# A Strassen scheme for the down projection of a TensorE-bound attention and MLP-Mixer kernel

## The chip, the cores and the metric

The kernel runs on one core of one Trainium2 chip. The metric is the device time of that core in microseconds. Spans and waits come from a profiled execution, which is some 2 us shorter than the timed figure (304.3 us of span beside 306.4 us of time). Runs are compared when their granted TensorE clock says that they are in the same state.

## The reference

Eight batches go through block-causal attention (8 heads, 576 positions, head width 64) and then through one MLP-Mixer layer: a token mix across positions and a channel mix with an inner width of 1536.

```python
x  = attention(q, k, v)                       # [8, 576, 512]
h  = relu(x.T @ w_tok1) @ w_tok2              # token mix, per batch
u  = x + h.T
h2 = relu(u @ w_ch1) @ w_ch2                  # channel mix: 512 -> 1536 -> 512
out = u + h2                                  # float32
```

The last product, `relu(...) @ w_ch2`, is the **down projection**. Per batch it is [512 rows x 1536] @ [1536 x 512]; the last 64 rows of two neighbouring batches are handled together as a "pair" of 128 rows ("mixed" in the code).

## The kernel before: what the change touches

The kernel first makes a list of operations, each with its engines, an assumed cost, its dependencies and the buffers it takes. A planner replays this list on a small model of the engines, moves priorities at random 1000 times from a fixed seed, keeps what ends earliest, and then emits every engine's instructions in the order found, with semaphore waits where one needs another engine's result. So an edit to the list of operations also starts the search anew.

```python
def search(self, tries):
    rnd = random.Random(0)
    ...
    for _ in range(tries):
        moved = list(prios)
        ...
        end = run(moved)[0]
        if end <= best:
            best, prios = end, moved
    return run(prios)[1]
```

The channel mix keeps the hidden activations transposed, `gT` = [128 partitions, 12 channel chunks, 512 rows], which makes them the stationary operand of the down projection. Each chunk of 128 rows is 12 matmuls of 512 columns, accumulated in one PSUM bank, and one eviction by VectorE that adds the residual:

```python
for n, si in enumerate(chunks):               # 4 chunks of 128 rows
    ...
    for cols in (slice(0, 256), slice(256, 512)) if last else (slice(0, 512),):
        ...
        for part in range(3):
            ...
            for cc in range(4 * part, 4 * part + 4):
                nc.tensor.matmul(
                    out=ps, lhsT=gt[:, cc, c0 : c0 + 128], rhs=wc2_sb[:, cc, cols],
                    start=(cc == 0 and not turned), stop=(cc == NDC - 1),
                )
        ...
        nc.vector.tensor_tensor(
            out=dst, in0=ps, in1=(ut if mixed else ut[:, si, :])[:, cols], op=ADD
        )
```

Batch 0 differs ("turned"): its residual is added on TensorE by identity matmuls in the same bank. The program sets up four "mm" banks of PSUM for all of this and two double banks for attention's scores.

The softmax here doesn't subtract the row's maximum and nothing guards it: scores larger than these inputs give would overflow.

## Time and profile before

| | before |
|---|---|
| time, median of runs | 306.38 us (306.02 to 306.77) |
| span of the profiled run | 304.3 us |
| TensorE busy | 296.9 us, 98% |
| VectorE busy | 155.5 us, 51% |
| ScalarE busy | 164.6 us, 54% |
| granted TensorE clock | 1.000 |

The page's other lines are in the prediction. How they are read: a digit of the slices is the busy share of a fortieth of the span in tenths; a group has line, engine, operation, tiles and shapes, then the count, busy time and mean ns of one, then the engine's idle time before it and what ended that.

### The profile page before, as it was taken

The numbers are of one execution on the slowest core, as the hardware profiler recorded it, in microseconds if no ns is written. First come the engines' busy times: TensorE is split into PE (matmuls) and PEld (weight loads), VectorE is DVE, ScalarE is ACT, GpSimd is POOL, SyncE is SP. The second block draws the span as 40 slices with busy tenths as digits, with TensorE's granted clock in tenths as the row PEclk, the third lists the DMA queues.
The fourth block names the chain that finished last, engine by engine and source line by source line (L and its number), as shares of the span: only waits on it lengthen the run. The fifth ranks groups of instructions, "written<-read, shape, count | busy, mean of one in ns | idle before, by whom it ended". The sixth has DMA issues, their size and how long they took to land.

```text
span 304.3 us, 7056 instructions
## 1 busy us (share of the span) xinstructions
PE 296.9 (98%) x2999; PEld 160.7 (53%) x3034; DVE 155.5 (51%) x380; ACT 164.6 (54%) x233; POOL 62.1 (20%) x96
## 2 busy tenths in 40 slices
PE   8999999999999999999999999999999999999995
PEld 4575456465454564555554564645446545555443
DVE  5566539989595599584987253615023021010112
ACT  5887855677855756875557856324413503615300
POOL 9766454702610602600140000000000000000000
PEclk9999999999999999999999999999999999999999
DMA  8999999995982998975193002033113222100133
GB/s 202 179 196 209 200 191 187 220 216 91 142 121 44 161 119 139 189 46 60 54 107 88 2 2 53 18 95 97 36 32 140 46 80 49 43 26 2 69 138 106
DMA packets 64383, 31.94 MB, mean 105 GB/s; under 512 B 53088, under 2 KB 55008, under 8 KB 64352
## 3 DMA queue, kind: packets, MB, share of 16 engines
q0 software_dynamic: 44320, 17.34, 48.9%
q1 hardware_dynamic: 19744, 13.57, 17.1%
q10 hardware_dynamic: 288, 0.59, 0.5%
q8 instruction: 23, 0.38, 0.5%
q14 instruction: 8, 0.07, 0.1%
HBM read 35.85 MB, written 9.44 MB: 149 GB/s over the span
## 4 chain that ended last, share of the span: by engine, by line
PE 95%; DMA 2%; issue 1%; DVE 1%; ACT 0%; ACTq 0%
PE mm L1031 31%; PE mm L947 28%; PE mm L555 10%; PE sc L508 10%; PE mm L736 6%; PE mm L829 4%; PE mm L974 4%; DMA gT<-in_q_dram 2%; PE mm L860 1%; PE mm L332 1%; PE mm L780 0%; PE mm L910 0%; DVE qT L393 0%; PE mm L1023 0%; PE mm L765 0%
## 5 line engine op out<-in xcount | busy, mean ns | idle before, releaser
L527 ACT ACTIVATE e_sb<-sc 128x1024 bf16<-128x1024 f32 x95 | 92.5, 1028 | 26.3 <-PE sc L508 24.5
L947 PE MATMUL mm<-uT,wc_sb 128*128 128x512 bf16 x384 | 91.2, 380 | 0.1
L1031 PE MATMUL mm<-wc_sb,gT 128*128 128x512 bf16 (+1 forms) x372 | 89.4, 372 | 1.5 <-issue 0.5
L722 ACT ACTIVATE gT<-mm 128x512 bf16<-128x512 f32 x74 | 44.2, 597 | 63.1 <-PE mm L947 62.8
L947 PEld LDWEIGHTS <-wc_sb 128*128 128x128 bf16 x384 | 41.9, 114 | 39.3 <-issue 3.9
L1031 PEld LDWEIGHTS <-gT 128*128 128x128 bf16 x396 | 36.9, 98 | 40.8 <-issue 3.3
L1056 DVE TENSOR_TENSOR o_sb<-mm,u_sb 128x512 f32<-128x512 f32 (+1 forms) x29 | 19.5, 672 | 74.5 <-PE mm L1031 74.3
L422 POOL DMA_DIRECT2D v<-in_v_dram x45 | 37.2, 839 | 35.3 <-PE sc L508 23.6
L508 PE MATMUL sc<-qT,kT 32*128 32x64 bf16 (+4 forms) x744 | 35.4, 281 | 0.5 <-DVE qT L393 0.5
L555 PEld LDWEIGHTS <-e_sb 128*128 128x128 bf16 x896 | 31.1, 97 | 8.0 <-issue 3.6
L555 PE MATMUL mm<-v,e_sb 128*128 128x65 bf16 x896 | 33.9, 193 | 0.1
L583 DVE TENSOR_TENSOR x_sb<-mm,rinv 128x320 bf16<-128x320 f32 x64 | 31.0, 491 | 2.0
L724 DVE TENSOR_SCALAR gT<-mm 128x512 bf16<-128x512 f32 x22 | 15.2, 689 | 15.9 <-PE mm L947 15.7
L844 DVE TENSOR_TENSOR u_sb<-mm,x_sb 128x512 bf16<-128x512 f32 x28 | 18.0, 686 | 10.2 <-PE mm L829 9.0
L393 DVE STREAM_TRANSPOSE qT<-qraw 128x288 int32<-128x288 int32 x32 | 21.6, 706 | 3.0 <-PE sc L508 2.1
L393 DVE STREAM_TRANSPOSE kT<-kraw 128x288 int32<-128x288 int32 x32 | 20.9, 703 | 4.3 <-DMA kraw<-in_k_dram 1.7
L508 PEld LDWEIGHTS <-kT 32*128 32x128 bf16 x752 | 12.3, 93 | 19.8 <-issue 16.7
L736 PE MATMUL mm<-x_sb,w_sb 128*128 128x512 bf16 (+1 forms) x98 | 18.0, 314 | 0.3
L533 DVE MEMSET e_sb<- 64x128 uint32 (+1 forms) x72 | 10.5, 153 | 14.7 <-ACT e_sb L527 11.4
L373 POOL DMA_DIRECT2D qraw<-in_q_dram x15 | 8.3, 552 | 42.2 <-DVE qT L393 28.5
L577 DVE RECIPROCAL rinv<-mm 128x5 f32<-128x5 f32 x64 | 11.4, 185 | 7.4 <-PE mm L555 6.7
L722 ACT ACTIVATE aT<-mm 128x512 bf16<-128x512 f32 (+1 forms) x15 | 8.1, 543 | 12.3 <-PE mm L736 12.3
(66 smaller groups left out, 175.6 us busy)
## 6 DMA issues: line engine op xcount, KB each, us to landing
out_dram<-o_sb SPq DMA_DIRECT2D x15, 512.0 KB, 2.9
kraw<-in_k_dram POOLq DMA_DIRECT2D x15, 288.0 KB, 7.7
qraw<-in_q_dram POOLq DMA_DIRECT2D x15, 288.0 KB, 7.2
v<-in_v_dram POOLq DMA_DIRECT2D x28, 128.0 KB, 6.9
wc_sb<-in_moe_w_ch_dram POOLq DMA_DIRECT2D x8, 192.0 KB, 7.1
wc_sb<-in_moe_w_ch_dram POOLq DMA_DIRECT2D x3, 512.0 KB, 10.4
out_dram<-o_sb SPq DMA_DIRECT2D x10, 128.0 KB, 2.3
v<-in_v_dram POOLq DMA_DIRECT2D x15, 64.0 KB, 6.1
```

Source lines behind the costliest of these rows:

```text
L393: nc.vector.transpose(dst[:, 0:S, :] .rearrange("p s e -> p (s e)") .bitcast(I32) .rearrange("p (a k) -> p k a", k=NB)[:, k0:k1], raw2.bit ...
L422: nc.gpsimd.dma_start(out=dst, in_=src)
L508: nc.tensor.matmul(out=home(n)[:, c0 : c0 + w], lhsT=kT[i][r, j0 : j0 + 128, par], rhs=qT[i][r, i0 : i0 + w, par], start=(par == 0), stop= ...
L527: nc.scalar.activation(dst, sc[SC.index(note["pool"])][:, :, 0:n], EXP, scale=scale)
L555: nc.tensor.matmul(out=u[:, I, 0:65], lhsT=w, rhs=vt[:, J, head, 0:65], start=(J == 0), stop=(J == I),)
L583: nc.vector.tensor_tensor(out=xt[:, :, 64 * head : 64 * head + 64], in0=u[:, :, 0:64], in1=ri.to_broadcast([128, 5, 64]), op=MULT,)
L722: nc.scalar.activation(dst, src, RELU)
L736: nc.tensor.matmul(out=bank_of(bank)[:, w * n : w * n + w], lhsT=wt[:, tt : tt + 255 : 2], rhs=xt[:, c, cols], start=(c == 0), stop=(c == 4),)
L844: nc.vector.tensor_tensor(out=ut[:, si, :], in0=bank_of(bank), in1=xt[:, si, :], op=ADD)
L947: nc.tensor.matmul(out=bank_of(bank), lhsT=wc1_sb[:, m, channels(cc)], rhs=uT[b % 2][:, :, m, :], start=(m == 0), stop=(m == NDM - 1),)
L1031: nc.tensor.matmul(out=ps, lhsT=gt[:, cc, c0 : c0 + 128], rhs=wc2_sb[:, cc, cols], start=(cc == 0 and not turned), stop=(cc == NDC - 1),)
L1056: nc.vector.tensor_tensor(out=dst, in0=ps, in1=(ut if mixed else ut[:, si, :])[:, cols], op=ADD)
```

## The change

The intent is to give TensorE less to do. Chunks t and t+2 of a batch (rows 128t and 128t+256) are taken as two row blocks, the channels as two halves of 768, the output columns as two halves of 256. That is a 2 x 2 by 2 x 2 block product, which Strassen's scheme (in Winograd's form) does in 7 block products, not 8:

- sums of activations, on VectorE, per chunk pair: s1 = a21 + a22, s2 = s1 - a11, s4 = a12 - s2, s3 = a11 - a21 (s3 in place of a21);
- differences of weights, on VectorE, once: w1 to w4;
- seven products of 6 matmuls with 256 columns each;
- three PSUM banks: in bank "a" four products pile up one after the other, and after each of them VectorE folds the bank's present content into one quarter of the output tile; bank "e" holds two products, bank "c" one.

The residual is added in the first fold of each quarter, from the chunk pair's own rows. Batches 1 to 7 are changed; batch 0 and the pairs are not. With the new tiles, two rings of the pairs (`umT`, `gmT`) shrank from two buffers to one each, and the zeros for the filler matmuls in the first 16 us moved into the new weights' tile.

The diff, cut to its core (the rest changes buffer indices):

```diff
-    umT = ring(2, [128, NDM, 128], BF16, "umT")
+    umT = ring(1, [128, NDM, 128], BF16, "umT")
-    gmT = ring(2, [128, NDC, 128], BF16, "gmT")
+    gmT = ring(1, [128, NDC, 128], BF16, "gmT")
+    sums = ring(3, [128, 3, NDC // 2, 128], BF16, "sums")
-    zeros = sb.tile([128, 512], BF16, name="zeros")
+    wd_sb = sb.tile([128, 4, NDC // 2, 256], BF16, name="wd_sb")
+    zeros = wd_sb[:, 0, 0:2, :].rearrange("p c s -> p (c s)")
+    def weight_sums(wc2_ready):
+        ...                                    # 4 differences of [128, 6, 256]
+    def channel_down_fast(b, g_done, wc2_ready, u_done, prio):
+        for t in range(2):
+            ...
+            for key, dst, x, y, op in (
+                ("s1", s1, a21, a22, ADD), ("s2", s2, s1, a11, SUB),
+                ("s4", s4, a12, s2, SUB), ("s3", a21, a11, a21, SUB),
+            ):
+                def emit(o, dst=dst, x=x, y=y, op=op):
+                    nc.vector.tensor_tensor(out=dst, in0=x, in1=y, op=op)
+            ...
+            def product(n, to, x, y, deps):
+                bank, first = banks[to], to not in last
+                def emit(o):
+                    for kk in range(H6):
+                        nc.tensor.matmul(
+                            out=bank_of(bank)[:, 0:256], lhsT=x[:, kk], rhs=y[:, kk],
+                            start=first and kk == 0, stop=kk == H6 - 1, ...
+                        )
+                # waits for the fold before it in the same bank: deps + [last.get(to)]
+            def fold(to, row, col, op, residual, final):
+                other = ut[:, t + 2 * row, cols] if residual else dst
+                nc.vector.tensor_tensor(out=dst, in0=bank_of(bank)[:, 0:256], in1=other, op=ADD)
+            fold("a", 0, 0, product(0, "a", a11, b11, []), True, False)
+            fold("e", 1, 1, product(1, "e", s1, w1_, [made["s1"]]), True, False)
+            fold("a", 0, 1, product(2, "a", s2, w2_, [made["s2"]]), True, False)
+            fold("e", 0, 1, product(3, "e", s4, b22, [made["s4"]]), False, True)
+            fold("a", 1, 1, product(4, "a", a21, w3_, [made["s3"]]), False, False)
+            fold("c", 0, 0, product(5, "c", a12, b21, []), False, True)
+            fold("a", 1, 0, product(6, "a", a22, w4_, []), True, True)
-            if p < B - 1:
+            if p == 0:
                 channel_down(p, ...)
+            elif p < B - 1:
+                channel_down_fast(p, ...)
```

More of the change, by code (lines that the diff above doesn't have):

```diff
@@ L19 @@
 MULT = mybir.AluOpType.mult
+SUB = mybir.AluOpType.subtract
 class Op:
@@ L897, in emit @@
             def emit(o):
-                nc.sync.dma_start_transpose(out=umT[pair % 2], in_=umt)
-            op = P.add("SP", 1.0, emit, um_rows + reuse(("umT", pair % 2)), prio, xfer=1.0)
+                nc.sync.dma_start_transpose(out=umT[0], in_=umt)
+            op = P.add("SP", 1.0, emit, um_rows + reuse(("umT", 0)), prio, xfer=1.0)
             reads(("um", pair % 2), op)
@@ L914, in token_mix @@
             deps = ([u_done[si]] if si < 4 else um_rows) + pads["ident"]
-            deps += uT_war if si < 4 else reuse(("umT", pair % 2))
+            deps += uT_war if si < 4 else reuse(("umT", 0))
             op = P.add(
@@ L922, in emit @@
                 ps = bank_of(bank).bitcast(BF16)[:, 0:512].rearrange("p (m s) -> p m s", m=NDM)
-                dst = uT[b % 2][:, si] if si < 4 else umT[pair % 2]
+                dst = uT[b % 2][:, si] if si < 4 else umT[0]
                 if o.engine == "ACT":
@@ L964, in channel_up_mixed @@
     def channel_up_mixed(pair, umT_done, wc1_ready, prio):
-        g_war = reuse(("gm", pair % 2))
+        g_war = reuse(("gm", 0))
         done = []
@@ L976, in emit @@
                             lhsT=wc1_sb[:, m, channels(cc)],
-                            rhs=umT[pair % 2][:, m, :],
+                            rhs=umT[0][:, m, :],
                             start=(m == 0),
@@ L982, in channel_up_mixed @@
             op = P.add("PE", mm_cost(128, 16), emit, umT_done + wc1_ready[4 * f] + g_war, prio + 0.1 * f, take=[(BANK, bank)])
-            reads(("umT", pair % 2), op)
+            reads(("umT", 0), op)
             def emit(o, f=f, bank=bank):
@@ L987, in emit @@
                     o,
-                    gmT[pair % 2][:, 4 * f : 4 * f + 4, :],
+                    gmT[0][:, 4 * f : 4 * f + 4, :],
                     bank_of(bank).rearrange("p (c s) -> p c s", c=4),
@@ L993, in channel_up_mixed, with emit @@
         return done
+    H6 = NDC // 2
+    wd_ready = []
+    def weight_sums(wc2_ready):
+        b11, b12 = wc2_sb[:, 0:H6, 0:256], wc2_sb[:, 0:H6, 256:512]
+        b21, b22 = wc2_sb[:, H6:NDC, 0:256], wc2_sb[:, H6:NDC, 256:512]
+        t = [wd_sb[:, n] for n in range(4)]
+        for dst, x, y, deps in (
+            (t[0], b12, b11, wc2_ready), (t[2], b22, b12, wc2_ready), (t[1], b22, t[0], []), (t[3], b21, t[1], [])
+        ):
+            def emit(o, dst=dst, x=x, y=y):
+                nc.vector.tensor_tensor(out=dst, in0=x, in1=y, op=SUB)
+            wd_ready.append(P.add("DVE", 0.9, emit, deps + wd_ready[-1:], 14.0))
@@ new lines, in channel_down_fast, with emit @@
+    def channel_down_fast(b, g_done, wc2_ready, u_done, prio):
+        gt, ut = gT[b % 2], u_sb[b % 3]
+        for t in range(2):
+            oi = out_n[0] % 3
+            out_n[0] += 1
+            o_war = reuse(("o", oi))
+            si = sum_n[0] % 3
+            sum_n[0] += 1
+            s_war = reuse(("s", si))
+            r1, r2 = slice(128 * t, 128 * t + 128), slice(128 * t + 256, 128 * t + 384)
+            a11, a12 = gt[:, 0:H6, r1], gt[:, H6:NDC, r1]
+            a21, a22 = gt[:, 0:H6, r2], gt[:, H6:NDC, r2]
+            s1, s2, s4 = (sums[si][:, n] for n in range(3))
+            made = {}
+            prev = None
+            for key, dst, x, y, op in (
+                ("s1", s1, a21, a22, ADD), ("s2", s2, s1, a11, SUB), ("s4", s4, a12, s2, SUB), ("s3", a21, a11, a21, SUB),
+            ):
+                def emit(o, dst=dst, x=x, y=y, op=op):
+                    nc.vector.tensor_tensor(out=dst, in0=x, in1=y, op=op)
+                prev = made[key] = P.add(
+                    "DVE", dve_cost(768, 2), emit, (g_done + s_war if prev is None else [prev]), prio - 2 + 0.1 * t
+                )
+                reads(("g", b % 2), prev)
+            b11, b21, b22 = wc2_sb[:, 0:H6, 0:256], wc2_sb[:, H6:NDC, 0:256], wc2_sb[:, H6:NDC, 256:512]
+            w1_, w2_, w3_, w4_ = (wd_sb[:, n] for n in range(4))
+            banks = {"a": {}, "c": {}, "e": {}}
+            last = {}
+            stored = []
+            def product(n, to, x, y, deps):
[4 more added lines that the diff above has]
+                            out=bank_of(bank)[:, 0:256], lhsT=x[:, kk], rhs=y[:, kk],
+                            start=first and kk == 0, stop=kk == H6 - 1,
+                            skip_group_check=not first,
+                        )
+                op = P.add(
+                    "PE", mm_cost(256, H6), emit, deps + g_done + wc2_ready + wd_ready + [last.get(to)],
+                    prio + 0.2 * t + 0.02 * n, take=[(BANK, bank)] if first else (),
+                )
+                reads(("g", b % 2), op)
+                reads(("s", si), op)
+                last[to] = op
+                return op
+            def fold(to, row, col, op, residual, final):
+                dst = o_sb[oi][:, row, 256 * col : 256 * col + 256]
+                bank = banks[to]
+                other = ut[:, t + 2 * row, 256 * col : 256 * col + 256] if residual else dst
+                def emit(o):
+                    nc.vector.tensor_tensor(out=dst, in0=bank_of(bank)[:, 0:256], in1=other, op=ADD)
+                done = P.add(
+                    "DVE", dve_cost(256), emit, [op, folded.get((row, col))] + u_done + o_war, prio - 1,
+                    give=[bank] if final else (),
+                )
+                reads(("u", b % 3), done)
+                folded[row, col] = last[to] = done
+                return done
+            folded = {}
+            fold("a", 0, 0, product(0, "a", a11, b11, []), True, False)
[5 more added lines that the diff above has]
+            fold("a", 1, 0, product(6, "a", a22, w4_, []), True, True)
+            rows = out[b, 0:512, :].rearrange("(c t p) d -> t p c d", c=2, t=2)[t]
+            if b == B - 1 and t == 1:
+                pieces = [(0, 0, 2), (1, 1, 2), (1, 0, 1)]
+            else:
+                pieces = [(None, 0, 2)]
+            for row, c0, c1 in pieces:
+                def emit(o, row=row, c0=c0, c1=c1, oi=oi, rows=rows):
+                    cols = slice(256 * c0, 256 * c1)
+                    if row is None:
+                        nc.sync.dma_start(out=rows, in_=o_sb[oi])
+                    else:
+                        nc.sync.dma_start(out=rows[:, row, cols], in_=o_sb[oi][:, row, cols])
+                deps = [folded[r, c] for r in ((0, 1) if row is None else (row,)) for c in range(c0, c1)]
+                size = (2 if row is None else 1) * (c1 - c0) / 2
+                reads(("o", oi), P.add("SP", 0.5, emit, deps, prio, xfer=8 * 0.086 * size))
@@ L995 @@
     out_n = [0]
+    sum_n = [0]
     def channel_down(b, g_done, wc2_ready, u_done, prio, mixed=False):
         chunks = [None] if mixed else list(range(4))
-        gt = gmT[b // 2 % 2] if mixed else gT[b % 2]
+        gt = gmT[0] if mixed else gT[b % 2]
         ut = um_sb[b // 2 % 2] if mixed else u_sb[b % 3]
@@ L1046, in channel_down @@
                     )
-                reads(("gm", b // 2 % 2) if mixed else ("g", b % 2), prev)
+                reads(("gm", 0) if mixed else ("g", b % 2), prev)
                 if turned:
@@ L1098 @@
     wc1_ready, wc2_ready = load_channel_weights()
+    weight_sums(wc2_ready)
     x_done = {}
@@ L1112 @@
             g_done = channel_up(p, uT_done, wc1_ready, 10 * p + 2)
-            if p < B - 1:
+            if p == 0:
                 channel_down(p, g_done, wc2_ready, u_done, 10 * p + 4)
+            elif p < B - 1:
+                channel_down_fast(p, g_done, wc2_ready, u_done, 10 * p + 4)
             if p % 2 == 1:
@@ L1119 @@
             if p == B - 1:
-                channel_down(p, g_done, wc2_ready, u_done, 10 * p + 4)
+                channel_down_fast(p, g_done, wc2_ready, u_done, 10 * p + 4)
     with tc.manual_schedule():
```

## The prediction

No row of the kernel before shows the new sums, so their times in the prediction are estimates. The same figures can be worked out from rows of that kernel, the 690 and 424 ns of 512 and 256 f32 columns in the prediction and these two:

```profile
L355 DVE COPY o_sb<-mm 128x512 f32<-128x512 f32 x2 | 1.4, 691 | 0.1
L927 DVE COPY uT<-mm 128x512 bf16<-128x512 bf16 x3 | 1.2, 422 | 1.1 <-PE mm L910 1.1
```

From 690 and 424 ns an f32 column takes (690 - 424)/256 = 1.039 ns, and 158 ns come on top. The bf16 copy of 512 columns takes 422 ns, as long as 256 f32 columns: double rate. If the bf16 sums show it too, 768 columns take an estimated 158 + 384 x 1.039 = 557 ns and 1536 take 956; at single rate 768 take 956.

> **What bounds the kernel now.** I read first the busy shares and the 40 slices of the page, then the chain that ended last, then the groups with shapes kept apart, then the waits of TensorE alone and the timeline of the end.
>
> Busy shares, slices, chain and the waits of TensorE alone, from the kernel before:
>
> ```profile
> PE 296.9 (98%) x2999; PEld 160.7 (53%) x3034; DVE 155.5 (51%) x380; ACT 164.6 (54%) x233; POOL 62.1 (20%) x96
> ...
> PE   8999999999999999999999999999999999999995
> ...
> DVE  5566539989595599584987253615023021010112
> ...
> PEclk9999999999999999999999999999999999999999
> ...
> PE 95%; DMA 2%; issue 1%; DVE 1%; ACT 0%; ACTq 0%
> ...
> PE mm L1031 <- issue: 0.5, 3, 0.2
> PE sc L508 <- DVE qT L393: 0.5, 1, 0.5
> ```
>
> TensorE (PE) is busy 98% of the 304.3 us span in every slice but the first and last, makes up 95% of the chain, and, after its start, waited for another engine under 1 us in all. Its clock was 1.000. So the kernel takes as long as TensorE's instruction stream: a microsecond out of that stream is a microsecond off the time, as long as no new wait appears. VectorE (DVE) is half busy on the average, but the slices show two different halves: mostly 5 to 9 tenths up to slice 25 (attention still running), 0 to 3 after. That matters below.
>
> The groups that the change touches (line, engine, operation, tiles, shapes, count | busy us, mean ns), and rows of the timeline (start, us):
>
> ```profile
> L1031 PE MATMUL mm<-wc_sb,gT 128*128 128x512 bf16 x348 | 86.6, 379 | 1.5 <-issue 0.5
> L1031 PE MATMUL mm<-wc_sb,gT 128*128 128x256 bf16 x24 | 2.8, 272 | 0.0
> L1056 DVE TENSOR_TENSOR o_sb<-mm,u_sb 128x512 f32<-128x512 f32 x27 | 18.6, 690 | 73.0 <-PE mm L1031 72.8
> L1056 DVE TENSOR_TENSOR o_sb<-mm,u_sb 128x256 f32<-128x256 f32 x2 | 0.8, 424 | 1.5 <-PE mm L1031 1.5
> ```
>
> ```profile
> 209.08 5.34 PE L947 MATMUL mm<-uT,wc_sb 128*128 128x512 bf16 x24
> ...
> 298.18 2.78 PE L1031 MATMUL mm<-wc_sb,gT 128*128 128x256 bf16 x24
> ...
> 301.00 0.42 DVE L1056 TENSOR_TENSOR o_sb<-mm,u_sb 128x256 f32<-128x256 f32 x1 [0.89 <-PE mm L1031]
> ```
>
> A matmul's mean of 379 or 272 ns is its latency, not its cost: they are pipelined. The pace comes from runs. 24 matmuls of 512 columns took 5.34 us: (5.34 - 0.379)/23 = 0.2157 us each. 24 of 256 columns, each with its own weight load, took 2.78 us: (2.78 - 0.272)/23 = 0.1090 us each. So a 256-column matmul costs 0.505 of a 512-column one, and its weight load stays hidden. This is what the Strassen scheme lives on, since all its products are 256 columns wide.
>
> [...]
>
> **The change, part by part.**
>
> Removed on TensorE: batches 1 to 7 have 4 chunks x 12 matmuls of 512 columns each, where the last chunk of batch 7 is split in halves: 324 of 512 and 24 of 256 columns: 324 x 0.2157 + 24 x 0.1090 = 72.5 us. Added: 7 batches x 2 chunk pairs x 7 products x 6 = 588 of 256 columns: 588 x 0.1090 = 64.1 us. Net **-8.4 us**, all on the path. (A full seventh/eighth of 72.5 would be -9.1[...].) The built streams confirm the 588 and leave every other TensorE group as it was: both kernels visit the score matmuls 59 times, so the 0.24 us or so that entering and leaving such a visit costs (0.67 us from matmul to matmul around a visit at 127.7 us, against 0.43 for its columns) does not change.[...]
>
> VectorE. Removed: 26 evictions of 512 and 2 of 256 columns of batches 1 to 7, about 19 us. Added: 98 folds of 256 columns at 0.424 = 41.6 us; 56 sums of activations at an estimated 0.557 = 31.2 us; four sums of weights of 1536 elements, estimated 0.96 each, 3.8 us, once. Net +57 us: VectorE goes from 155 to about 213 us, 71% of the span. Not the bound on the average. ScalarE and the transfers stay as they are; output bytes are the same.
>
> New dependencies. Products now share banks in chains: product, fold into the output, next product on top in the same bank, which must wait for the fold. From the end of one product's issue the bank is back after 0.163 (latency less pace) + 0.04 (matmul end to eviction start at 301.00) + 0.424 + about 0.1 for the signal back (my allowance) = 0.73 us. One product in between is 6 x 0.109 = 0.65 us: alone, not enough. I went through TensorE's built order and added up, at these paces, the work between one product and the next in the same bank: 69 times a product follows another there; the smallest gap is 0.80 us, 7 are below 1 us, most are 1.3 us (two products between) or more. So with VectorE free, almost no chain waits.
>
> But VectorE is a queue. With starts of consecutive operations some 0.08 us closer than their durations (two 512-wide evictions took 1.29 us where one takes 0.69) I summed VectorE's own order from a batch's first sum to its last fold, against TensorE's work from that batch's first to last product: batch 1: 14.6 of VectorE in 15.9 of TensorE; 2: 15.2 in 15.9; 3: 16.7 in 20.3; 4: 8.6 in 10.0; 5: 9.2 in 11.8; 6: 8.6 in 9.2; 7: 9.2 in 10.9. VectorE can start its sums somewhat before the first product, so each fits, but batches 1 and 2 are at over 90% with attention's reciprocals, normalisations and transposes in the same queue. There I expect short waits: I put **+1.6 us** in all (1.0 for batches 1 to 3, 0.4 for the rest, 0.2 for the start). This is a judgement, not a sum. For batch 7 I followed the order by hand: last activation at 0.9 us after its matmuls, eight sums at 0.475 end at 4.75, the folds of the first products end by 5.5, and TensorE comes back to those banks at 5.4 us or later: no loss worth counting.
>
> The tail is the same: last product, one 256-column fold (0.42), 128 KB out. 306.4 - 8.4 + 1.6 = **299.6 us**, a gain of 2.2%.
>
> **Rivals.** (a) VectorE keeps up wholly: 298.0 us. For it: before, TensorE waited for almost nothing although VectorE was at 80% in some stretches; the order was searched for. (b) The sums run at single rate: 56 x 0.4 = 22 us more of VectorE, batches 1 and 2 go over 100% of their windows, and each batch's first sums come 3 us late: 10 us of new waits or more, 306 to 310 us. Against it: [...] the 16-bit copy out of PSUM shows double rate in this trace (512 columns in 422 ns). (c) VectorE becomes the bound of batches 1 to 3 only, in a queue stuck behind transposes that wait for loads: 3 to 5 us of waits, 301.5 to 303 us. The 91% to 96% of two windows speaks for it; that a late stretch may catch up does not help, since TensorE has no slack anywhere. (d) Narrow matmuls with weights changing each time run slower than in the one run of 24 seen at the end, say 0.113 (the pace of the weight loads there): +2.4 us, 302 us. The longest run seen speaks against it.
>
> **Range and chances.** (a) and the central case lie on one side of 2% (300.25 us), (c) and (d) on the other; the centre is only 0.65 us from it. Range 297.4 to 303.0. Faster by over 2%: 0.62; within: 0.35; slower: 0.03, nearly all of it (b).
>
> **What would show it.** The group of the products: 588 matmuls, mean 272 ns, pace 0.109 in the chain; TensorE busy or stream shorter by 8.4 us. Sums at 0.55 us (double rate) and not 0.95. VectorE near 213 us. Waits of TensorE for VectorE's folds: under 2 us in total if I am right, 3 to 5 and in the windows of batches 1 to 3 if (c) is. Score visits and the start unchanged within 0.5 us. I would be wrong if TensorE's waits are large in the last third, where VectorE has room, or if the start or the score visits have changed length by more than a microsecond through the new order.

## More of the kernel before

One view more, because the experiments come back to it: three stretches of the kernel before. Columns are the stretch, its length, then busy us (and instructions) of TensorE, its weight loads, VectorE, ScalarE and GpSimd, then the granted clock, the transfer share and GB/s.

```profile
80.00:100.00 20.00, 19.79 (x236) 10.04 (x238) 14.08 (x34) 12.87 (x17) 3.80 (x6) 1.00 0.89 92
140.00:160.00 20.00, 19.63 (x265) 10.48 (x268) 14.56 (x37) 10.60 (x13) 4.20 (x5) 1.00 0.77 85
260.00:280.00 20.00, 19.89 (x128) 11.15 (x129) 2.08 (x3) 8.41 (x15) 0.00 (x0) 1.00 0.07 27
```

In the two stretches with attention VectorE is 70% and 73% busy, in the late one 10%. TensorE is full in all three.

## The result

The changed kernel took **298.92 us** (median, 298.65 to 299.19), the kernel before 306.57 in the same rounds (306.02 to 306.82): 7.65 us less. The ratio is 0.9749 with a 95% interval of 0.9732 to 0.9767: faster by 2.5%. Ratios are the mean time of one kernel's fast runs over that of the other's of the same rounds, so not quite the ratio of the medians. Its result is correct against the reference.

The page of the changed kernel: busy shares, slices, chain by engine.

```profile
PE 290.8 (98%) x3257; PEld 184.7 (62%) x3276; DVE 203.7 (69%) x509; ACT 164.4 (55%) x233; POOL 62.0 (21%) x96
...
PE   8999999999999999999999999999999999999995
...
DVE  5566879899679979959988787665086085028284
...
PEclk9999999999999999999999999999999999999999
...
PE 95%; DMA 2%; DVE 1%; ACT 1%; issue 1%; ACTq 0%
```

TensorE is as full as before, and the chain is as much TensorE's: the bound has not moved, its stream has become shorter. VectorE went from 51% to 69%, most visibly in the last third, where mostly zeros to threes became peaks of 8.

What TensorE waited for in the changed kernel, and the groups that answer to those shown before:

```profile
PE mm L328 <- DVE wd_sb L299: 1.2, 1, 1.2
PE sc L511 <- DVE qT L396: 0.3, 1, 0.3
```

```profile
L1071 DVE TENSOR_TENSOR o_sb<-mm,u_sb 128x256 f32<-128x256 f32 x56 | 23.1, 420 | 7.7 <-PE mm L1049 6.8
L1049 PE MATMUL mm<-wc_sb,gT 128*128 128x256 bf16 x168 | 22.0, 273 | 0.0
L1049 PE MATMUL mm<-wd_sb,gT 128*128 128x256 bf16 x168 | 21.9, 273 | 0.0
L1049 PE MATMUL mm<-wd_sb,sums 128*128 128x256 bf16 x168 | 21.4, 273 | 0.0
L1071 DVE TENSOR_TENSOR o_sb<-mm,o_sb 128x256 f32<-128x256 f32 x42 | 17.4, 421 | 7.5 <-PE mm L1049 7.1
L1032 DVE TENSOR_TENSOR sums<-gT,sums 128x768 bf16<-128x768 bf16 x14 | 7.4, 549 | 0.0
L1049 PE MATMUL mm<-wc_sb,sums 128*128 128x256 bf16 x84 | 11.3, 273 | 0.0
```

The products are all there (168 x 3 + 84 = 588), with a latency of 273 ns, where 256 columns had 272 before. No matmul is recorded as waiting for a fold or a sum; among the weight loads, which run ahead of the matmuls (at 289.95 us for the run of 12 at 290.06 below), three short waits for VectorE at the products add up to 1.0 us:

```profile
PEld L1049 <- DVE e_sb L536: 0.4, 1, 0.4
PEld L1049 <- DVE gT L1032: 0.4, 1, 0.4
PEld L1049 <- DVE o_sb L1071: 0.2, 1, 0.2
```

The narrow pace shows in a run near the end, 12 matmuls in 1.47 us:

```profile
290.06 1.47 PE L1049 MATMUL mm<-wd_sb,gT 128*128 128x256 bf16 x12
```

A sum takes 549 to 555 ns (means of its four kinds) for 768 bf16 columns, where 512 f32 columns take 690: the double rate that the prediction estimated (557).

The same three stretches of the changed kernel as shown before:

```profile
80.00:100.00 20.00, 20.00 (x279) 13.26 (x278) 16.71 (x42) 13.59 (x19) 2.37 (x4) 1.00 0.76 79
140.00:160.00 20.00, 19.89 (x244) 13.10 (x244) 18.18 (x46) 12.76 (x15) 4.19 (x5) 1.00 0.66 82
260.00:280.00 20.00, 20.00 (x159) 14.76 (x158) 9.31 (x22) 7.39 (x13) 0.00 (x0) 1.00 0.15 54
```

VectorE rose to 84% and 91% in the crowded stretches and from 10% to 47% in the late one, and TensorE stayed full in all three.

**Where the 7.4 us of span came from.** I cut both runs at the first channel-up matmul, at the end of the last score visit, and at the end of the last matmul's issue, and set beside each stretch the sum of the matmuls that TensorE's built stream has there, at paces found as in the prediction. (The built stream is used because the trace lacks some records: the page before counts 2999 matmuls, but 3034 weight loads.)

| stretch | before: trace, sum of paces | changed: trace, sum of paces | overhead gained |
|---|---|---|---|
| to the first channel-up matmul | 26.8 us | 27.1 us | +0.3 |
| to the end of the scores | 163.8, 153.0 | 165.1, 153.8 | +0.5 |
| to the last matmul's issue | 110.2, 109.9 | 101.1, 100.7 | +0.1 |
| end (fold and transfer) | 3.5 | 3.6 | +0.1 |

From the first channel-up matmul on, the sum of the paces fell by 8.4 us; of this 1.0 us came back as a slightly later start and small overheads, half of it while attention runs.

### The profile page after: what moved, and what is told of

Read it like the earlier page. It is cut to its first block, busy times and chain, and to the rows that moved or that the text cites.

```text
span 296.9 us, 7686 instructions
## 1 busy us (share of the span) xinstructions
PE 290.8 (98%) x3257; PEld 184.7 (62%) x3276; DVE 203.7 (69%) x509; ACT 164.4 (55%) x233; POOL 62.0 (21%) x96
## 4 chain that ended last, share of the span: by engine, by line
PE 95%; DMA 2%; DVE 1%; ACT 1%; issue 1%; ACTq 0%
PE mm L950 28%; PE mm L1049 22%; PE mm L558 10%; PE sc L511 10%; PE mm L1144 7%; PE mm L739 6%; PE mm L832 4%; PE mm L977 4%; DMA gT<-in_q_dram 2%; PE mm L863 1%; ACT e_sb L530 1%; PE mm L783 1%; PE mm L335 0%; PE mm L913 0%; DVE u_sb L847 0%
## 5 line engine op out<-in xcount | busy, mean ns | idle before, releaser
L950 PE MATMUL mm<-uT,wc_sb 128*128 128x512 bf16 x384 | 89.6, 380 | 0.0
L1049 PEld LDWEIGHTS <-gT 128*128 128x128 bf16 x336 | 32.0, 98 | 6.7 <-issue 1.7
L1032 DVE TENSOR_TENSOR sums<-gT 128x768 bf16<-128x768 bf16 x14 | 7.2, 555 | 36.4 <-ACT gT L725 36.4
L1071 DVE TENSOR_TENSOR o_sb<-mm,u_sb 128x256 f32<-128x256 f32 x56 | 23.1, 420 | 7.7 <-PE mm L1049 6.8
L1049 PEld LDWEIGHTS <-sums 128*128 128x128 bf16 x252 | 24.3, 98 | 5.6 <-DVE e_sb L536 0.4
L1071 DVE TENSOR_TENSOR o_sb<-mm,o_sb 128x256 f32<-128x256 f32 x42 | 17.4, 421 | 7.5 <-PE mm L1049 7.1
L1049 PE MATMUL mm<-wc_sb,gT 128*128 128x256 bf16 x168 | 22.0, 273 | 0.0
L1049 PE MATMUL mm<-wd_sb,gT 128*128 128x256 bf16 x168 | 21.9, 273 | 0.0
L1049 PE MATMUL mm<-wd_sb,sums 128*128 128x256 bf16 x168 | 21.4, 273 | 0.0
L727 DVE TENSOR_SCALAR gT<-mm 128x512 bf16<-128x512 f32 x20 | 13.8, 688 | 7.6 <-PE mm L950 7.2
```

Of the source, the lines that this page charges most:

```text
L950: nc.tensor.matmul(out=bank_of(bank), lhsT=wc1_sb[:, m, channels(cc)], rhs=uT[b % 2][:, :, m, :], start=(m == 0), stop=(m == NDM - 1),)
L1049: nc.tensor.matmul(out=bank_of(bank)[:, 0:256], lhsT=x[:, kk], rhs=y[:, kk], start=first and kk == 0, stop=kk == H6 - 1, skip_group_check= ...
L1071: nc.vector.tensor_tensor(out=dst, in0=bank_of(bank)[:, 0:256], in1=other, op=ADD)
```

## The experiments

The theory: the time is TensorE's instruction stream, and the gain is the work taken out of it, as long as VectorE delivers sums and folds in time. Rivals: the new search made the gain; the smaller rings or the moved zeros did; narrow matmuls eat part of it; VectorE has ample room, or has none. Twelve kernels ran, in three groups, each group on one chip with the kernel before beside it (medians 306.56, 306.53 and 306.47 us).

| run | median us (all runs) | ratio to before, 95% interval |
|---|---|---|
| kernel before, other seed | 312.76 (307.64 to 313.9) | three runs slow, no ratio |
| changed, other seed | 299.65 (299.6 to 299.79) | 0.9769 (0.9735 to 0.9803) |
| changed, plain down projection | 306.48 (306.36 to 306.61) | 0.9991 (0.9962 to 1.002) |
| before, in 256 columns | 308.45 (307.98 to 310.04) | 1.0065 (1.0025 to 1.0104) |
| scheme in batches 4 to 7 | 302.58 (301.82 to 302.72) | 0.9861 (0.9843 to 0.988) |
| scheme in batches 1 to 3 | 304.3 (303.88 to 304.45) | 0.9924 (0.9907 to 0.994) |
| sums made twice, old order | 328.7 (326.48 to 329.52) | 1.0706 (1.0664 to 1.0749) |
| no sums (wrong result) | 298.44 (298.08 to 298.91) | 0.9732 (0.9714 to 0.9749) |
| changed, again | 298.75 (298.27 to 299.38) | 0.9738 (0.9719 to 0.9757) |
| sums made twice, planner told | 312.18 (311.68 to 313.09) | 1.0182 (1.016 to 1.0205) |
| scheme in batch 0 too | 303.58 (303.18 to 304.59) | 0.9904 (0.9885 to 0.9923) |
| the same, longer search | 301.18 (300.84 to 301.7) | 0.9822 (0.9802 to 0.9841) |

### Is it the order? Other seeds

```diff
-        rnd = random.Random(0)
+        rnd = random.Random(1)
```

The kernel before from another seed:

> The kernel before, its schedule searched from another random seed. Theory (the time is TensorE's instruction stream, and the order found by the search hardly matters): 305.7 to 307.5 us, within 0.4% of before. Rival (much of the change's 7.65 us is luck of the search, which started anew when the list of operations changed): differs from before by more than 2 us.

The changed kernel from another seed:

> The changed kernel from another seed. Theory: 298 to 300 us, again 7 to 8.5 us under the kernel before with its seed 1; TensorE waits for VectorE's folds under 1 us in all. Rival (luck of the search): 301 us or more, or under 297.

The changed kernel with the other seed is at 299.65 us, 0.7 to 0.9 above its runs with the first seed. The kernel before with the other seed has one run in the fast state, 307.64 us; its three others have a mean granted clock of 0.972 to 0.976 and are not compared. What slowed them is in the stretches of the profiled one:

```profile
8.00:10.00 2.00, 1.41 (x28) 0.77 (x26) 0.09 (x1) 1.05 (x2) 1.66 (x3) 1.00 1.31 165
10.00:12.00 2.00, 1.69 (x17) 0.74 (x17) 1.55 (x5) 2.00 (x5) 0.54 (x1) 1.00 1.66 171
12.00:14.00 2.00, 2.00 (x28) 1.25 (x27) 1.55 (x5) 2.00 (x7) 1.82 (x3) 0.58 1.48 197
24.00:26.00 2.00, 2.00 (x28) 1.89 (x27) 0.80 (x3) 1.02 (x1) 1.52 (x3) 0.51 1.15 203
```

After a start in which TensorE was busy 1.41 and 1.69 us of 2, the clock (third figure from the end) went to about half for more than 12 us; the three slow runs took 4.9 to 6.3 us more than the fast one. In the profiled run that loss lies in the start: its first channel-up matmul comes at 32.1 us, where the kernel before with its own seed has 26.8, and from there to the last matmul it takes 274.4 us beside 274.0. The same order once ran at full clock, so the order alone does not decide it; but no run of the kernel before with its own seed showed it. So an order can cost several microseconds, in some executions, through the clock, which the planner does not model. At full clock the orders differed by about a microsecond. The gain, 7.65 us with the first seeds and 8.0 with seed 1 (there against a single fast run), is not luck of the search; but a microsecond of any difference between two kernels here can be. My expectation for the kernel before (305.7 to 307.5) was missed even by the fast run, by 0.1.

### Is it what came along? The plain down projection in the changed kernel

```diff
-    weight_sums(wc2_ready)
...
-                channel_down_fast(p, g_done, wc2_ready, u_done, 10 * p + 4)
+                channel_down(p, g_done, wc2_ready, u_done, 10 * p + 4)
```

> The changed kernel with the plain down projection of the kernel before for batches 1 to 7, but with all that the change did besides: one buffer in place of two for the 64-row pairs, zeros laid into the weight sums' tile. Theory (the gain is the seventh product saved and nothing else): 305.7 to 307.5 us, as before. Rival (the smaller rings or the new layout moved the time): off from before by over 1.5 us.

306.48 us: with the smaller rings and the moved zeros, but the old eight products, the time of the kernel before is back to 0.1 us. The whole gain is the scheme's.

### What do narrow matmuls cost? Eight products in halves

```diff
-            for cols in (slice(0, 256), slice(256, 512)) if last else (slice(0, 512),):
+            for cols in (slice(0, 256), slice(256, 512)) if last or (b > 0 and not mixed) else (slice(0, 512),):
```

> The kernel before with all eight block products, but each down projection of batches 1 to 7 in 256-column halves: 672 matmuls of 256 columns in place of 324 of 512 and 24 of 256, and 56 evictions of 256. Theory (a 256-column matmul with its own weight load costs 0.109 us against 0.2157): 672 x 0.1090 - 72.5 = +0.75 us, so 306.8 to 308 us. Rival (narrow matmuls with changing weights cost 0.113 or more, so the scheme's saving was eaten there): 309.5 us or more. The distance from this run to the changed kernel is then the eighth product alone: 84 x 0.109 = 9.2 us less waits.

The three runs at a clock of 1.000 took 307.98 to 308.46 us, so going to 256 columns cost 1.4 to 1.9 us where the sum of the paces gives 0.75: the median, 308.45, misses the expected range by half a microsecond. The pace itself held:

```profile
301.82 3.22 PE L1031 MATMUL mm<-wc_sb,gT 128*128 128x256 bf16 x28
```

(3.22 - 0.272)/27 = 0.1092 us each. The fourth run, the profiled one, is slower by its clock: the first channel-up matmul comes at 29.2 us, with the clock at 0.50 between 14 and 16 us. The rest of the cost, 0.7 to 1.2 us, is about what two orders differ by, and a single order cannot tell it from twice as many evictions. The step from this kernel to the changed one, 308.4 to 298.9, is 9.5 us, against 84 x 0.109 = 9.2 for the product saved. Read this way, the saved product brought all that it should, and what is missing from 8.4 us was lost with the halving, before the scheme; both statements carry the microsecond of the orders.

### Late batches or early ones?

```diff
-            elif p < B - 1:
+            elif p < 4:
+                channel_down(p, ...)
+            elif p < B - 1:
                 channel_down_fast(p, ...)
```

(and the reverse for the other run)

> The scheme for batches 4 to 7 only, whose down projections run when attention is over or nearly; batches 1 to 3 plain. TensorE's stream is 4 x 1.2 = 4.8 us shorter than before. Theory (each batch pays what its TensorE stream loses, wherever it runs; waits small): 301.5 to 302.8 us. Rival (the late half, where VectorE has room, brings nearly the whole gain and the early half none): 299.5 or less, close to the changed kernel.

> The scheme for batches 1 to 3 only, in the stretch where attention fills VectorE too. TensorE's stream is 3 x 1.2 = 3.6 us shorter. Theory: 302.7 to 304.2 us (3.6 less 0.3 to 0.9 of waits and order). Rival (in the crowded stretch the folds cost what the product saves): 305.5 us or more.

Four late batches bring 3.95 us of 4.8, three early ones 2.2 us of 3.6. In the profiled runs, from the first channel-up matmul to the last matmul, the late kernel gained 4.3 us over before and the early one 2.6. Both late and early batches pay; the early ones lose about 1.0 us of what they save, the late ones about 0.5, from TensorE's stream to the trace. Together they bring 6.2 us and not 7.65: each kernel has its own order, so the microsecond of the orders is in these figures too, and half a microsecond between early and late is not shown to be attention's. The early run was 0.1 above its range: its tail, from the last matmul to the end, was half a microsecond longer. The rival that the crowded stretch gives nothing is refuted (it said 305.5 or more).

### How much room has VectorE? Sums made twice, in the old order

```diff
                 def emit(o, dst=dst, x=x, y=y, op=op):
+                    nc.vector.tensor_tensor(out=spare, in0=x, in1=y, op=op)
                     nc.vector.tensor_tensor(out=dst, in0=x, in1=y, op=op)
```

The planner did not know of it: TensorE's built stream is identical to the changed kernel's, and VectorE's differs by the 56 added instructions only.

> The changed kernel with every sum of activations made twice, the first into a spare tile that nobody reads (the result stays right): same order on TensorE and on VectorE, each sum takes twice the 0.475 us that it takes of VectorE's queue[...]. 56 x 0.475 = 27 us more of VectorE. Theory (VectorE's windows were 82 to 96% full, by the sums of the prediction): six of the seven windows go over 100%, by 14.7 us together, less what the sums' early start gives back: 305 to 312 us. Rival (VectorE has so much room that its added work is free): 298.5 to 300.5 us.

It took 328.7 us: 29.8 us more for 56 x 0.475 = 27 us of VectorE. Both theories named too small a cost. The timeline of batch 1's window shows how:

```profile
95.38 0.63 PE L512 MATMUL sc<-qT,kT 32*128 32x320 bf16 x16
...
98.07 0.55 DVE L1033 TENSOR_TENSOR spare<-gT 128x768 bf16<-128x768 bf16 x1
98.65 0.56 DVE L1034 TENSOR_TENSOR gT<-gT 128x768 bf16<-128x768 bf16 x1
99.29 0.17 DVE L537 MEMSET e_sb<- 64x128 uint32 x1
99.49 0.76 DVE L1073 TENSOR_TENSOR o_sb<-mm,u_sb 128x256 f32<-128x256 f32 x2
99.97 1.44 PE L1051 MATMUL mm<-wd_sb,sums 128*128 128x256 bf16 x6 [3.96 <-DVE o_sb L1073]
```

The first folds of a batch stand in VectorE's queue behind all eight sums. In the changed kernel they begin at 95.44 us, just when TensorE needs the banks back (its next product in them starts at 95.92):

```profile
95.44 0.75 DVE L1071 TENSOR_TENSOR o_sb<-mm,u_sb 128x256 f32<-128x256 f32 x2
```

Here they begin at 99.49, and TensorE waits 3.96 us, about the eight added sums (8 x 0.475 = 3.8). Over the whole run it waited for folds twelve times:

```profile
PE mm L1051 <- DVE o_sb L1073: 20.4, 12, 4.0
```

TensorE does not sit idle for what overfills the window, it sits idle for what stands ahead of the fold. After the long gap the clock was at 0.51 from 98 to 105 us, and the run's mean clock is 0.978 over 327.7 us of span: at most some 7 us by estimate (0.022 x 327.7) came on top of the waits.

### Does TensorE wait for sums in the changed kernel? No sums

```diff
-            s1, s2, s4 = (sums[si][:, n] for n in range(3))
+            s1, s2, s4 = a12, a11, a22
...
-                prev = made[key] = P.add("DVE", dve_cost(768, 2), emit, ...)
+                made[key] = None
```

> WRONG RESULT ON PURPOSE: the changed kernel without the sums of activations (the products read the plain blocks), same 588 products and 98 folds, 31 us less of VectorE, and no product waits for a sum. The changed kernel keeps 7.4 us of span out of 8.4. Theory (the missing 1.0 us is 0.3 of a longer start and 0.7 of order and waits for folds, hardly for sums): 298.3 to 299.3 us. Rival (the missing microsecond is products waiting for sums): 297.5 to 298.2 us.

298.44 us, 0.3 to 0.5 under the changed kernel's two medians and in the theory's range, with less of VectorE:

```profile
PE 291.6 (98%) x3269; PEld 184.1 (62%) x3269; DVE 180.4 (61%) x455; ACT 163.4 (55%) x231; POOL 62.0 (21%) x96
```

So 23 us of VectorE's busy time (204 less 180) cost 0.3 to 0.5 us, which is less than two orders differ by. The sums are hidden; the missing microsecond is not mainly theirs.

### Queue or capacity? The sums twice, and the planner told

```diff
-                    "DVE", dve_cost(768, 2), emit, ...
+                    "DVE", 2 * dve_cost(768, 2), emit, ...
```

This together with the doubled sums above.

> The sums made twice again, but with the planner told that they cost twice as much, so that it searches an order for them. With the old order the doubling cost 29.8 us for 27 us of added VectorE. Theory (VectorE has room on the average, 230 us of 300, and what cost so much is its queue: all eight sums of a batch stand ahead of the folds that the placed products wait for): most of it comes back, 299.5 to 304 us. Rival (capacity: a batch's window on VectorE is simply full): 312 us or more.

312.18 us. The search took back 16.5 us of the 29.8, so more than half was the order. But 13.4 us over the control remain, in the range that my rival, capacity, had named, and near the 14.7 us of overfull windows in the expectation of the doubled sums (its 'six of the seven' and '82 to 96%' are slips: by the prediction's figures the windows were 78 to 96% full, and 14.7 us is the sum of all seven overflows). What TensorE waited for:

```profile
PE mm L1051 <- DVE o_sb L1073: 3.2, 6, 1.0
PE mm L1051 <- DVE sums L1034: 3.2, 1, 3.2
PE mm L1051 <- DVE gT L1034: 2.3, 1, 2.3
```

8.7 us of waits for folds and sums that do not exist in the changed kernel, and a mean clock of 0.993. The wait of 3.2 us shows a full window: until 270.1 us VectorE had stood idle for 11.4 us, waiting for the last batch's activations, then it was busy 9.0 us of 9.1, with folds between the sums, and TensorE waited meanwhile. So a VectorE that is 73% busy over the span can be the bound in a single window. That capacity makes all of the 13.4 us is not shown: a longer search, which found 2.4 us in the next kernels, was not tried on this one.

### A step further? Batch 0 too, and a longer search

```diff
-            if p == 0:
-                channel_down(p, ...)
-            elif p < B - 1:
+            if p < B - 1:
                 channel_down_fast(p, ...)
...
+        for si in range(4 if b == 0 else 0):      # batch 0: turn uT back into u
+            ...                                   # 4 identity matmuls a chunk, evicted into ut[:, si, :]
```

The control in the same rounds, then the two kernels (the second with 2,500 tries of the search for 1,000):

> The changed kernel unaltered, as the control of these rounds: 298.6 to 299.3 us.

> The scheme for batch 0 too: its residual, until now added on TensorE by 16 identity matmuls into each chunk's bank, is turned by the same 16 matmuls into the residual tile first, which takes 4 more evictions. TensorE's stream gets 48 x 0.2157 - 84 x 0.109 = 1.2 us shorter than the changed kernel's. Theory (TensorE's stream sets the time): 297.3 to 298.6 us, faster than the control by 0.4 to 1.5 us. Rival (at 40 to 60 us VectorE is already 86% busy, the four sums of weights now have to come before the first products, so waits or a longer start eat it): 299 us or more.

> The same with 2,500 tries of the search for 1,000. Theory (the orders found are close to TensorE's bound already; what differs between them is the start, 26.6 to 27.7 us, and some tenths of waits): within 0.6 us of the run with 1,000 tries. Rival (the search is what limits): over 1 us faster than it.

303.58 us, 4.8 us slower than the control at 298.75, though TensorE's stream is 1.2 us shorter (all its runs have a mean clock of 0.989 to 0.994, so its clock is part of the effect); the rival was right, and more than it had said. Stretches and waits of that run:

```profile
40.00:44.00 4.00, 3.74 (x88) 2.41 (x85) 3.89 (x11) 3.42 (x5) 3.56 (x6) 1.00 1.49 196
44.00:48.00 4.00, 0.63 (x15) 0.40 (x12) 3.77 (x12) 1.94 (x2) 0.82 (x2) 1.00 1.55 194
48.00:52.00 4.00, 4.00 (x64) 3.63 (x61) 3.35 (x11) 0.00 (x0) 1.09 (x2) 0.57 1.40 195
52.00:56.00 4.00, 3.95 (x30) 2.88 (x30) 3.66 (x8) 0.60 (x1) 3.45 (x5) 1.00 1.58 101
```

```profile
PE mm L558 <- DVE e_sb L536: 3.4, 2, 1.8
```

From 40 to 48 us VectorE is busy 3.9 and 3.8 us of each 4, with weight sums, activation sums and normalisations. Behind them in its queue stand two memsets of 0.17 us that mask attention's exponentials, and TensorE's value matmuls wait for these: it is busy 0.63 us of 4. Over the next 4 us the clock is 0.57. So what stood ahead of two memsets of 0.17 us cost TensorE over 3 us; that the lower clock in the next 4 us came from it is not shown. The longer search found an order without that gap (301.18 us, clock 0.999), 2.4 us better than 1,000 tries and so another rival right, but still slower than the control: VectorE is 19.4 us of 20 busy between 40 and 60 us there. No kernel tried that gives the right result beats the changed one. A batch-0 version with its sums spread out stays open.

## Why the prediction was right

The prediction said 299.6 us; 298.92 and 298.75 were measured.

- **TensorE's stream, -8.4 us.** Held. The built streams differ by that sum, the latency of the narrow matmul was the 273 ns seen before, and a run of 12 of them near the end took 1.47 us, (1.47 - 0.273)/11 = 0.109 us each. An eighth of the 72.5 us would be 9.1; two matmuls of 256 columns take 2.3 ns more than one of 512 (2 x 109.0 beside 215.7), and 294 such pairs take 0.7 back. The plain kernel with all of the change's other parts is back at 306.48.
- **Double rate of the sums.** Held: 543 to 559 ns for 768 columns against the estimate of 557. The weight differences of 1536 columns took 949 to 958 ns against the estimate of 960.
- **VectorE's total.** 203.7 us busy, not 213. The step "net +57 us" added durations; consecutive operations overlap by some 0.08 us, as the same prediction says two paragraphs later, so 48 was the rise; the eight sums of a batch, 549 ns each, start 0.47 us apart. (Two small slips: 27 evictions of 512 columns went, as its own line shows, not 26; and after slice 25 of VectorE stand a 6 and a 5 before the zeros to threes. Neither moves the time.)
- **Waits, +1.6 us, called a judgement.** The term was too large: the table of stretches gives 1.0 us (0.3 start, 0.5 up to the end of the scores, 0.2 after), and the medians 0.75. That it is waits for VectorE is not shown: no matmul is recorded as waiting for a fold or a sum, half of the 1.0 us lies where attention fills VectorE, and without the sums the time fell by 0.3 to 0.5 us, within the scatter of orders.
- **Bank chains.** Right: with gaps of 0.80 us and more against 0.73 needed, TensorE shows no wait of a matmul for a fold. The 0.1 us for the signal back was an allowance; in the doubled sums, where a product did wait, its fold started at 99.49 us and took 0.42, and the product started at 99.97, 0.06 us after.
- **Rival (a), 298.0 us,** was nearly as close as the centre, and its mechanism, a VectorE that keeps up, fits the recorded waits better. Another seed alone moves the changed kernel by 0.7 to 0.9 us, so which of the two numbers came closer is luck. **Rival (d)** fell: the pace of 0.113 was not seen (0.109 in the run of 12). **Rival (c)** fell as well: the crowded batches lost about 1.0 us, not 3 to 5.
- **Rival (b), single rate, 306 to 310 us,** was mis-sized as a rival. The doubled sums, which take about the time of single rate (2 x 0.475 us of the queue beside the estimate of 0.956) but are two instructions, gave 328.7 us in the given order and 312.2 in an order made for them. The failing thought was to take a window's overfill for the cost. The cost in the fixed order was what stood ahead of the fold in the queue.

What stays open: how much of the last 0.7 to 1.0 us is the halving to 256 columns, how much VectorE and how much the order, since another seed alone moves either kernel by about a microsecond.

## What to carry to other kernels

When one engine's stream is the time, count its work before and after at the pace of runs in the trace, not at the latency of one instruction; that sum was right to within a microsecond here. Then check the helper engine by window and by place in its queue, not by its share of the span: 69% busy was harmless, 73% was not, and two memsets of 0.17 us behind a row of sums stopped the bound engine for 3.4 us. Where a random search sets the order, measure another seed before explaining a difference of a microsecond.

## What the runs show of TensorE's pace and clock

- Pace, at a clock of 1.000: 24 matmuls of 512 columns, with weight loads, have 215.7 ns each (5.34 us, kernel before); 24 of 256 columns, with a weight load each, 109.0 ns (2.78 us, the same kernel).
- Clock: the amount of idle time alone does not decide when it falls. In the batch-0 run it was 0.57 between 48 and 52 us, after two gaps of 1.83 and 1.54 us with a little work between them. In the doubled sums TensorE was idle for 3.66 us of the 20 from 140 to 160 us, most of it around 151 us, and the clock was 1.00 in that stretch and in the next 20 us. In the kernel before with another seed it fell to 0.58 and stayed near half for over 12 us although TensorE was busy 1.41 and 1.69 us of each 2 us before; the same program once ran at 1.000. No run here shows what decides.
